# A positional-bias table for attention: order of its row groups, one-pass rows and early loads

## Chip, core and metric

The kernel runs on one core of one Trainium2 chip. The metric is the device time of one execution in microseconds (us). The core has a matrix engine (TensorE, PE in the rows), a vector engine (VectorE, DVE), a scalar engine (ScalarE, ACT), GpSimd (POOL) and a queue engine (SyncE, SP) that issues most transfers. Matmul results stand in PSUM, everything else on the chip in SBUF.

## What is computed

Attention with a learned positional bias, then a two-layer feed-forward block with a rational activation. Cut to what matters here:

```python
scores = scale * np.matmul(q, k.transpose(0, 1, 3, 2))        # B 4, H 8, S 576, D 64
psi_rel = np.log1p(np.abs(pos[:, None] - pos[None, :]))
psi_i = np.log1p(np.maximum(pos[:, None], 1.0))
x = (psi_rel / psi_i)[..., None]
bias = np.maximum(x @ w1 + b1, 0.0) @ w2                       # hidden 32, one value for each head
scores = scores + bias.transpose(2, 0, 1)[None]
attn = softmax(scores);  out = attn @ v
h = out @ w_in                                                 # 2304 x 512 @ 512 x 2048
P = a[0] + a[1]*h + a[2]*h**2 + a[3]*h**3
Q = 1 + abs(b[0])*abs(h) + abs(b[1])*h**2
result = (P / (Q + 1e-6)) @ w_out
```

The bias depends on the row i and on the distance |i-j| alone. With psi_i > 0 it is relu(w1 log1p(d) + b1 psi_i) @ w2 / psi_i.

## The kernel before

**Three stages.** First the bias table is made for all heads and written to DRAM (lines 571 to 680). Then attention runs in 72 steps over pairs of heads and batches, with the weights of the feed-forward block being split into high and low parts beside it. Then the feed-forward block runs (lines 701 to 884).

**The table.** The 576 rows i are cut into 36 *groups* of 16 rows (NROW). For a group n, `relu(n)` makes four *rows*: tiles of 128 partitions (32 hidden units times four values of i) by `dist(n)` columns, where `dist(n) = max(16n+16, 576-16n)` is the longest distance that the group needs, from 304 (the middle groups) to 576 (the first and the last). The letter in `ENG[n]` says who makes a row: D is one `tensor_scalar` on VectorE (line 617), A one activation on ScalarE (line 615). Before, a D row is max(x, -b), which lacks a constant; PE computes that constant once (`pc`, line 596), ScalarE copies it (`c8`), and it goes in as the bias of the activation below. Rows go through a ring of 18 tiles, and `relu` runs two groups ahead (LEAD).

For each group PE multiplies the four rows with the scaled w2 (`w28`, four 32-column parts that run side by side) into one PSUM tile `pb` of 591 columns (line 657). The PSUM tiles come from three slots, so group y waits until group y-3 has been read. ScalarE scales it into SBUF (`e`, line 663), and SP writes `e` (295.5 KB) to the table in DRAM (`tab<-e`, line 669). There are eight `e` tiles.

**From the table to attention.** The table of a pair of heads comes back in five *blocks* of 128 query rows (block c is the groups 8c to 8c+7, and block 4 has only the four groups 32 to 35). `load_bias(p, c)` issues three transfers for a block (line 261), and six for block 4: its 64 rows go to both halves of the partitions. `done` says behind which place y of the group order a block of the first pair is loaded. `step_a(0)` and `step_a(1)`, the first two attention steps, are issued between the last two groups (EARLY).

**A step of attention** on PE: scores `sc` (line 338), transposes `tp` of an earlier step (line 407), product with v `mx` (line 447). VectorE adds the bias block to `sc` and takes the row maximum (`s`, line 348), and ScalarE takes the exponential (`p`, line 364). The steps go (unit 0, block 0), (0, 1), (0, 2), (1, 0), (1, 1), (0, 3), (0, 4), ... `sc` has two PSUM buffers, both taken by one step, so step i+1 can't start on PE before `s` of step i has read. Unit 1 needs its own q and k (`q1`, `k1`): before, `loads(1)` issues them, and `v1`, from ScalarE's queue in `step_a(1)`.

Every engine takes its instructions in program order, and a wait holds up everything behind it on that engine. SP holds transfers in the order of the program too; each transfer has one of eight semaphores by turns, and waits until the transfer eight before it has landed.

## Time and profile before

| | us |
|---|---|
| median of 3 runs (lowest, highest) | 675.21 (674.49, 675.36) |
| the profiled execution | 675.17 |
| its span, first to last instruction | 673.4 |
| PE busy in the span | 665.0 (99%) |
| VectorE, ScalarE, GpSimd busy | 568.7, 484.3, 157.3 |
| mean granted clock of PE | 0.999 |

How the rows further down are read. A **stretch** row gives from:to in us from the start of the span, its length, then busy time (and count) of PE, PEld (PE's weight loads), DVE, ACT and POOL, PE's granted clock as a share of 2.4 GHz, the busy share of the 16 DMA engines, and GB/s. A **time line** row gives start, duration, engine, line, operation, what it writes<-reads, shapes and xcount; instructions of one kind in a row are merged, and the duration is then from the start of the first to the end of the last. In square brackets stands the engine's idle time before it and what ended that. Instructions of one engine overlap: the next starts before the one before it has ended. A **group** row gives line, engine, operation, shapes, count, then busy us, mean ns of one, and idle us before them. Engines with a q (SPq, ACTq) are their queues, issuing transfers. A **DMA** row ends with KB of one transfer and the median us from issue to landing. A busy PE is modelled, and is not PE at its peak.

### The profile page before, as it was taken

How to read it: one execution, taken by the hardware profiler on the slowest of the kernel's cores; microseconds unless marked ns; L12 is line 12 of the kernel's file. 1: busy time of each engine (PE TensorE's matmuls, PEld its weight loads, DVE VectorE, ACT ScalarE, POOL GpSimd, SP SyncE). 2: the span in 40 equal slices, each digit the busy share in tenths (PEclk: the TensorE clock that was granted, in tenths of full speed). 3: DMA queues.
4: the chain of work that ended last, by engine and by line, in shares of the span. 5: the costliest groups of instructions: out<-in, count | busy, mean ns of one | idle time of the engine just before them, and what ended most of it. 6: DMA issues, size and time to landing. Idle time of an engine off the chain costs nothing.

```text
span 673.4 us, 16639 instructions
## 1 busy us (share of the span) xinstructions
PE 665.0 (99%) x6468; PEld 575.2 (85%) x6468; DVE 568.7 (84%) x1072; ACT 484.3 (72%) x767; POOL 157.3 (23%) x117
## 2 busy tenths in 40 slices
PE   9998999999999999999999999999999999999997
PEld 5666888888888888999999999999999999999995
DVE  7985888888888896699999999998978787878776
ACT  6998889989888997676676767676655555555561
POOL 0000133334333232122222222222222222222221
PEclk9999999999999999999999999999999999999999
DMA  4997888698788974323635353679731212122021
GB/s 146 324 331 223 295 267 283 214 289 274 242 260 273 283 225 138 99 82 117 231 91 201 95 188 101 198 219 346 267 105 47 94 48 93 48 95 94 1 94 47
DMA packets 74702, 119.01 MB, mean 177 GB/s; under 512 B 11888, under 2 KB 33536, under 8 KB 74624
## 3 DMA queue, kind: packets, MB, share of 16 engines
q1 hardware_dynamic: 74048, 116.87, 53.1%
q10 hardware_dynamic: 576, 1.08, 0.6%
q8 instruction: 51, 0.84, 0.5%
q14 instruction: 27, 0.22, 0.1%
HBM read 79.17 MB, written 35.61 MB: 170 GB/s over the span
## 4 chain that ended last, share of the span: by engine, by line
PE 96%; DMA 2%; ACT 1%; issue 0%; DVEq 0%; DVE 0%; ACTq 0%
PE h L314 30%; PE o L793 29%; PE mx L447 13%; PE sc L338 12%; PE tp L407 5%; PE pb L657 5%; PE mx L407 1%; DMA k<-in_kt_dram 1%; DMA cst<-in_cst_dram 0%; DMA tab<-e 0%; ACT e L663 0%; ACT ring L615 0%; ACT p L364 0%; PE warm L597 0%; ACT pt L415 0%
## 5 line engine op out<-in xcount | busy, mean ns | idle before, releaser
L762 POOL TENSOR_TENSOR gl<-m,r 128x768 fp32r<-128x768 f32 x47 | 87.1, 1854 | 306.6 <-DVE m L755 281.9
L348 DVE CUSTOM_DVE_ANT_0 s<-sc,bias 128x576 f32<-128x576 f32 x144 | 103.2, 754 | 15.3 <-PE sc L338 10.1
L715 ACT ACTIVATE w<-h,babs 128x768 f32<-128x768 f32 x48 | 43.3, 902 | 99.5 <-PE h L314 99.5
L364 ACT ACTIVATE p<-s,m 128x576 f32<-128x576 f32 x144 | 110.7, 772 | 1.7 <-DVE m L348 1.1
L314 PE MATMUL h<-xh,wih 128*128 128x384 f32 x288 | 96.9, 336 | 0.0
L314 PE MATMUL h<-xh,wil 128*128 128x384 f32 x288 | 96.7, 336 | 0.0
L314 PE MATMUL h<-xl,wih 128*128 128x384 f32 x288 | 96.5, 335 | 0.0
L447 PE MATMUL mx<-pt,v 128*64 128x128 f32 (+1 forms) x1600 | 95.1, 267 | 0.0
L338 PE MATMUL sc<-k,q 64*128 64x288 f32 (+1 forms) x640 | 90.3, 426 | 2.2 <-DMA k<-in_kt_dram 1.5
L415 ACT COPY pt<-tp 128x1024 f32<-128x1024 f32 x72 | 72.6, 1008 | 24.8 <-PE tp L407 24.5
L793 PE MATMUL o<-wol,gh 128*128 128x512 f32 x216 | 84.7, 392 | 0.0
L793 PE MATMUL o<-woh,gh 128*128 128x512 f32 x216 | 84.6, 392 | 0.0
L447 PEld LDWEIGHTS mx<-pt,v 128*64 128x64 f32 x1600 | 78.5, 137 | 5.0 <-issue 0.2
L725 DVE SCALAR_TENSOR_TENSOR u<-w,babs,h 128x768 f32<-128x768 f32 x48 | 48.6, 1013 | 30.9 <-ACT t L716 30.9
L720 ACT ACTIVATE u<-u 128x768 f32<-128x768 f32 x48 | 40.7, 848 | 40.5 <-DVE u L725 40.5
L338 PEld LDWEIGHTS sc<-k,q 64*128 64x128 f32 (+1 forms) x640 | 49.5, 175 | 21.6 <-DVE m L348 6.9
L741 DVE SCALAR_TENSOR_TENSOR gh<-t,cst,r 128x768 fp32r<-128x768 f32 x48 | 48.7, 1015 | 9.5 <-ACT r L722 7.2
L314 PEld LDWEIGHTS h<-xh,wih 128*128 128x128 f32 x288 | 54.1, 188 | 1.8 <-issue 0.5
L314 PEld LDWEIGHTS h<-xl,wih 128*128 128x128 f32 x288 | 54.1, 188 | 1.3
L793 PE MATMUL o<-woh,gl 128*128 128x512 f32 x216 | 54.8, 389 | 0.0
L314 PEld LDWEIGHTS h<-xh,wil 128*128 128x128 f32 x288 | 54.0, 188 | 0.0
L748 DVE SCALAR_TENSOR_TENSOR m<-u,qc,gh 128x768 f32<-128x768 f32 x48 | 48.9, 1019 | 4.9
(79 smaller groups left out, 1270.3 us busy)
## 6 DMA issues: line engine op xcount, KB each, us to landing
tab<-e SPq DMA_DIRECT2D x36, 295.5 KB, 4.0
wx<-in_w_in_dram SPq DMA_DIRECT2D x16, 512.0 KB, 5.7
wx<-in_w_out_dram SPq DMA_DIRECT2D x16, 512.0 KB, 4.5
xr<-xd SPq DMA_DIRECT2D x7, 768.0 KB, 4.6
ws<-wh SPq DMA_DIRECT2D x20, 256.0 KB, 2.0
ws<-wl SPq DMA_DIRECT2D x20, 256.0 KB, 3.9
v<-in_vp_dram SPq DMA_DIRECT2D x15, 320.0 KB
bias<-tab SPq DMA_DIRECT2D x16, 288.0 KB, 4.0
```

Source lines behind the costliest of these rows:

```text
L314: T.matmul(hps[s][:, j, :TT], w[:, k, sl], x[:, k, :], start=(k == 0 and z == 0), stop=(k == KD - 1 and z == 2),)
L338: T.matmul(sc[i, j][o, a, :SH], q[r, x], k[r, a * SH:(a + 1) * SH], start=True, stop=True,)
L348: V.tensor_tensor_reduce(out=t.rearrange("p (a s) -> p a s", a=2), in0=sc.pop((i, j))[:, :, :SH], in1=bias[p][:, 5 * j + c, :].rearrange(" ...
L364: A.activation(out=prob[i][:, z * S:z * S + S], in_=t, func=AF.Exp, bias=m, scale=-1.0, accum_out=sums[u % 4][:, k:k + 1],)
L415: A.copy(out=t[:, 0:8].rearrange("p x (r s) -> p r x s", r=2), in_=ps)
L447: T.matmul(ps[y, o], vt[n][:, kc, y], t[:, 2 * kc + j if kc < 4 else 8, o], start=(kc == 0), stop=(kc == 4),)
L715: A.activation(out=w, in_=h, func=AF.Abs, scale=babs[:, 1:2])
L725: V.scalar_tensor_tensor(out=et(s, "u", 2), in0=rt[s, "w"], scalar=babs[:, 0:1], in1=hps[s][:, :, :TT], op0=ALU.add, op1=ALU.mult,)
L741: V.scalar_tensor_tensor(out=hi, in0=rt[s, "t"], scalar=abs_[:, 0:1], in1=rt[s, "r0"], op0=ALU.add, op1=ALU.mult,)
L748: V.scalar_tensor_tensor(out=m, in0=rt[s, "u"], scalar=qc, in1=rt[s, "gh"].bitcast(F32), op0=ALU.add, op1=ALU.mult,)
L762: eng.tensor_tensor(out=lo, in0=rt[s, "m"], in1=rt[s, "r0"], op=ALU.mult)
L793: T.matmul(po[n, c], l[:, j, c * P:(c + 1) * P], r[fp][:, j, :], start=(first and x is a), stop=(last and x is z),)
```

## The change

Five edits, all in the table stage and at its edge.

1. **Rows.** A D row is now max(x + b, 0), one `tensor_scalar` with two operations, and every row is complete. The constant (`pc`, `c8`, two small memsets and copies, the bias operand of `e`) is gone, and so is the second table `nts`; `bts` is made by VectorE.
2. **Who makes rows.** Groups with `dist` over 432 give all four rows to VectorE, those over 400 give one to ScalarE, the others two: 112 rows on VectorE and 32 on ScalarE, where there were 117 and 27.
3. **Order of the groups.** Before 0 to 15, 32 to 35, 16 to 31. Now a short group and a long one by turns, starting with the groups 16 and 17 and ending with 31, 24, 30, 25, 29, 26, 28, 27.
4. **Loads at the start.** The log table `lts` comes in two parts of 320 and 256 columns; `q0`, `k0`, `q1`, `k1` and `v0` are issued by SP right behind it, `v1` by SP at place 21.
5. **Loads of the bias blocks.** Before: block 0 behind place 10, 1 behind 18, 2 behind 30, 3 and 4 behind the last. Now: block 2 behind place 16, 0 behind 19, 4 behind 30, 1 behind 31, and 3 behind the last.

```diff
             def load_bias(p, c):
-                if c == 0:
+                if p not in bias:
...
             def loads(i):
                 g, c = divmod(i, UPG)
-                if i == 1:
-                    load_qk(1, nc.scalar)
-                    load_v(1, nc.scalar)
...
-                nc.sync.dma_start(out=lts, in_=ltab)
+                LCUT = 320
                 nc.scalar.dma_start(out=cs, in_=cst)
+                nc.sync.dma_start(out=lts[:, :LCUT], in_=ltab[:, :LCUT])
+                nc.sync.dma_start(out=lts[:, LCUT:], in_=ltab[:, LCUT:])
+                for u in range(2):
+                    load_qk(u)
+                load_v(0)
...
-                V.tensor_scalar(
-                    out=nts, in0=pts, scalar1=b1s, scalar2=-1.0, op0=ALU.mult, op1=ALU.mult
-                )
-                V.tensor_scalar(out=lts, in0=lts, scalar1=w1s, scalar2=None, op0=ALU.mult)
+                V.tensor_scalar(out=bts, in0=pts, scalar1=b1s, scalar2=None, op0=ALU.mult)
                 A.activation(out=w28, in_=cs[:, 8 + 5 * NG:], func=AF.Identity, scale=8.0)
-                A.activation(out=bts, in_=pts, func=AF.Identity, scale=b1s)
...
+                ENG = [
+                    "DDDD" if dist(n) > 432 else "DDDA" if dist(n) > 400 else "DDAA" for n in range(NG)
+                ]
...
                             V.tensor_scalar(
-                                out=r, in0=lts[:, :dist(n)], scalar1=nts[:, m:m + 1], scalar2=None,
-                                op0=ALU.max,
+                                out=r, in0=lts[:, :dist(n)], scalar1=bts[:, m:m + 1], scalar2=0.0,
+                                op0=ALU.add, op1=ALU.max,
                             )
...
-                done = {10: 0, 18: 1, 30: 2}
+                done = {16: 2, 19: 0, 30: 4, 31: 1}
...
-                    if y == 1:
-                        load_qk(0)
-                    if y == 4:
-                        load_v(0)
+                    if y == 21:
+                        load_v(1)
...
                     A.activation(
                         out=e, in_=pa.rearrange("p a s -> p (a s)")[:, :EW], func=AF.Identity,
-                        bias=c8[:, z:z + 1], scale=rts[:, n:n + 1],
+                        scale=rts[:, n:n + 1],
                     )
...
                     if y == NG - 1:
                         load_bias(0, 3)
-                        load_bias(0, 4)
```

**SP at the end of the table, before.** `e27` is the `e` tile of group 27, `tab2` the part of the table that block 2 reads, `bias0` the bias of the first pair of heads.

```order
L669 DMA tab3_70<-e26_797 128x591
L261 DMA bias0_393<-tab2_69 128x576
L261 DMA bias0_393<-tab2_69 128x512
L261 DMA bias0_393<-tab2_69 128x64
L669 DMA tab3_70<-e27_820 128x591
L669 DMA tab3_70<-e28_840 128x591
L669 DMA tab3_70<-e29_860 128x591
L669 DMA tab3_70<-e30_876 128x591
L669 DMA tab3_70<-e31_906 128x591
L261 DMA bias0_393<-tab3_70 128x576
```

The same place on SP in the changed kernel (x2 are two transfers in a row):

```order
L664 DMA tab3_69<-e30_797 128x591
L260 DMA bias0_511<-tab4_70 64x576 x2
L260 DMA bias0_511<-tab4_70 64x512 x2
L260 DMA bias0_511<-tab4_70 64x64 x2
L664 DMA tab3_69<-e25_823 128x591
L260 DMA bias0_511<-tab1_67 128x576
L260 DMA bias0_511<-tab1_67 128x512
L260 DMA bias0_511<-tab1_67 128x64
L664 DMA tab3_69<-e29_846 128x591
L664 DMA tab3_69<-e26_866 128x591
L664 DMA tab3_69<-e28_882 128x591
L664 DMA tab3_69<-e27_912 128x591
```

Block 4's six transfers have moved from behind the last group to a place five groups ahead of it, and block 1, which the second attention step reads, now stands behind them.

**ScalarE at the start of the table, before.** `ring` and `ring2` are row tiles, `pb0` is PE's result for group 0.

```order
L590 ACTIVATE w28_62<-cst_61 128x128
L591 ACTIVATE bts_137<-cst_61 128x144
L598 COPY c8_63<-pc_145 128x1
L599 COPY c8_63<-pc_145 96x1
L615 ACTIVATE ring_131<-lts_133,bts_137 128x576
L615 ACTIVATE ring_131<-lts_133,bts_137 128x560
L615 ACTIVATE ring2_132<-lts_133,bts_137 128x544
L663 ACTIVATE e0_184<-pb0_171,c8_63,cst_61 128x591
```

The same place on ScalarE in the changed kernel:

```order
L586 ACTIVATE w28_62<-cst_61 128x128
L612 ACTIVATE ring_130<-lts_132,bts_133 128x320 x2
L612 ACTIVATE ring_130<-lts_132,bts_133 128x304 x2
L658 ACTIVATE e16_188<-pb16_175,cst_61 128x591
L612 ACTIVATE ring2_131<-lts_132,bts_133 128x304 x2
L658 ACTIVATE e17_208<-pb17_195,cst_61 128x591
L658 ACTIVATE e0_228<-pb0_215,cst_61 128x591
L612 ACTIVATE ring_130<-lts_132,bts_133 128x320 x2
```

Three small instructions are gone from the head of ScalarE's queue, and its rows now come in pairs of short ones, with none between a short group's `e` and the long group's `e` behind it.

**ScalarE at the edge of attention, before.** `p0` is the exponential of step 0.

```order
L364 ACTIVATE p0_891,sum0_117<-s2_0_0_885,m0_0_886 128x576
L663 ACTIVATE e31_906<-pb31_893,c8_63,cst_61 128x591
L267 DMA q1_918<-in_qt_dram 128x576
L268 DMA k1_919<-in_kt_dram 128x576
L274 DMA v1_922<-in_vp_dram 128x640
L364 ACTIVATE p0_891,sum0_117<-s2_0_1_888,m0_1_889 128x576
```

In the changed kernel, ScalarE at the same place:

```order
L363 ACTIVATE p0_897,sum0_116<-s2_0_0_891,m0_0_892 128x576
L658 ACTIVATE e27_912<-pb27_899,cst_61 128x591
L363 ACTIVATE p0_897,sum0_116<-s2_0_1_894,m0_1_895 128x576
```

The three issues of unit 1's q, k and v have left ScalarE's queue; SP issues `q1` and `k1` at the very start.

## Rows read from the trace of the kernel before

**Rows 1.** The page, chain that ended last, share of the span by engine:

```profile
PE 96%; DMA 2%; ACT 1%; issue 0%; DVEq 0%; DVE 0%; ACTq 0%
```

**Rows 2.** Stretches: the table, attention from step 3, feed-forward, the end:

```profile
4.80:46.86 42.06, 41.96 (x840) 27.49 (x844) 42.04 (x117) 39.33 (x62) 0.45 (x1) 1.00 0.80 279
...
56.28:264.06 207.78, 207.78 (x3428) 173.00 (x3428) 176.21 (x530) 186.77 (x370) 66.71 (x53) 1.00 0.81 255
264.75:669.50 404.75, 404.73 (x2114) 367.27 (x2114) 343.84 (x407) 248.33 (x318) 88.53 (x48) 1.00 0.38 124
669.50:672.30 2.80, 0.00 (x0) 0.00 (x0) 0.86 (x2) 0.00 (x0) 0.00 (x0) 1.00 0.63 244
672.30:673.40 1.10, 0.00 (x0) 0.00 (x0) 0.00 (x0) 0.00 (x0) 0.00 (x0) 0.51 0.00 0
```

**Rows 3.** Time line of PE at the edge of attention:

```profile
50.24 1.32 PE L338 MATMUL sc<-k,q 64*128 64x288 f32 x8
52.33 1.67 PE L338 MATMUL sc<-k,q 64*128 64x288 f32 x7 [0.77 <-DVE m L348]
...
54.09 0.71 PE L407 MATMUL tp<-ident,p 64*128 64x64 f32 x13
56.28 1.24 PE L338 MATMUL sc<-k,q 64*128 64x288 f32 x8 [1.48 <-DMA k<-in_kt_dram]
...
59.25 1.24 PE L338 MATMUL sc<-k,q 64*128 64x288 f32 x8
```

**Rows 4.** Time line of VectorE at the edge of attention, step 1's first half:

```profile
51.51 0.76 DVE L348 CUSTOM_DVE_ANT_0 s<-sc,bias 128x576 f32<-128x576 f32 x1 [1.24 <-PE sc L338]
```

**Rows 5.** Time line of VectorE in the table stage:

```profile
4.04 0.29 DVE L586 TENSOR_SCALAR nts<-cst 128x144 f32<-128x144 f32 x1 [4.04 <-DMA cst<-in_cst_dram]
4.25 0.51 DVE L589 TENSOR_SCALAR lts<-lts,cst 128x576 f32<-128x576 f32 x1
4.80 42.04 DVE L617 TENSOR_SCALAR ring<-lts,nts 128x576 f32<-128x576 f32 x117
```

**Rows 6.** Groups of VectorE by shape, 0 to 50 us, longest and shortest rows:

```profile
L617 DVE TENSOR_SCALAR ring<-lts,nts 128x576 f32<-128x576 f32 x7 | 3.2, 520 | 0.0
...
L617 DVE TENSOR_SCALAR ring<-lts,nts 128x304 f32<-128x304 f32 x6 | 1.8, 386 | 0.0
```

**Rows 7.** Time line of ScalarE, start of the table:

```profile
8.82 0.84 ACT L663 ACTIVATE e<-pb,c,cst 128x591 f32<-128x591 f32 x1 [1.55 <-PE pb L657]
10.56 0.84 ACT L663 ACTIVATE e<-pb,c,cst 128x591 f32<-128x591 f32 x1 [0.90 <-PE pb L657]
11.30 0.71 ACT L615 ACTIVATE ring<-lts,bts 128x512 f32<-128x512 f32 x1
11.92 0.83 ACT L663 ACTIVATE e<-pb,c,cst 128x591 f32<-128x591 f32 x1
```

**Rows 8.** Time line of ScalarE, middle and end of the table:

```profile
30.98 0.61 ACT L615 ACTIVATE ring<-lts,bts 128x304 f32<-128x304 f32 x1
31.42 0.90 ACT L663 ACTIVATE e<-pb,c,cst 128x591 f32<-128x591 f32 x1
32.15 0.61 ACT L615 ACTIVATE ring<-lts,bts 128x304 f32<-128x304 f32 x1
...
43.49 0.95 ACT L663 ACTIVATE e<-pb,c,cst 128x591 f32<-128x591 f32 x1
...
46.14 2.42 ACT L663 ACTIVATE e<-pb,c,cst 128x591 f32<-128x591 f32 x3
```

**Rows 9.** Time line of SP's queue: a block of three, block 4 twice later:

```profile
9.69 0.32 SPq L669 DMA_DIRECT2D tab<-e  x1
...
44.97 1.29 SPq L261 DMA_DIRECT2D bias<-tab  x3
...
96.37 3.94 SPq L261 DMA_DIRECT2D bias<-tab  x6
...
150.47 4.20 SPq L261 DMA_DIRECT2D bias<-tab  x6
```

**Rows 10.** DMA issues from 44 to 46.9 us, the second of block 2's three:

```profile
bias<-tab SPq DMA_DIRECT2D x1, 256.0 KB, 4.5
```

**Rows 11.** Groups of PE by shape, 6.5 to 8 us, then 10.3 to 13 us:

```profile
L657 PE MATMUL pb<-ring,w 128*32 128x497 f32 x8 | 1.9, 1025 | 0.0
...
L657 PE MATMUL pb<-ring,w 128*32 128x465 f32 x8 | 1.0, 554 | 0.0
```

More of the change, by code (lines that the diff above doesn't have):

```diff
@@ L56, in tile_attn_moe @@
     w28 = cpool.tile([P, 4 * HID], F32, tag="w28", name="w28")
-    c8 = cpool.tile([P, 2], F32, tag="c8", name="c8")
     babs = cpool.tile([P, 2], F32, tag="babs", name="babs")
@@ L578, in tile_attn_moe @@
                 lts = tpool.tile([P, S], F32, tag="lts", name="lts")
-                nts = tpool.tile([P, NG * 4], F32, tag="nts", name="nts")
-                nc.sync.dma_start(out=lts, in_=ltab)
+                bts = tpool.tile([P, NG * 4], F32, tag="bts", name="bts")
+                LCUT = 320
                 nc.scalar.dma_start(out=cs, in_=cst)
-                bts = tpool.tile([P, NG * 4], F32, tag="bts", name="bts")
+                nc.sync.dma_start(out=lts[:, :LCUT], in_=ltab[:, :LCUT])
[3 more added lines that the diff above has]
+                load_v(0)
                 G.memset(qc, 1.0 + 1e-6)
                 G.memset(wmin, -8.0 * 0x38000000)
-                G.memset(c8, 0.0)
-                V.tensor_scalar(
-                    out=nts, in0=pts, scalar1=b1s, scalar2=-1.0, op0=ALU.mult, op1=ALU.mult
-                )
-                V.tensor_scalar(out=lts, in0=lts, scalar1=w1s, scalar2=None, op0=ALU.mult)
+                V.tensor_scalar(out=bts, in0=pts, scalar1=b1s, scalar2=None, op0=ALU.mult)
                 A.activation(out=w28, in_=cs[:, 8 + 5 * NG:], func=AF.Identity, scale=8.0)
-                A.activation(out=bts, in_=pts, func=AF.Identity, scale=b1s)
-                pc = ps_mx.tile([P, 2, 512], F32, tag="mx", name="pc")[:, 0]
+                for a, z in ((0, LCUT), (LCUT, S)):
+                    V.tensor_scalar(
+                        out=lts[:, a:z], in0=lts[:, a:z], scalar1=w1s, scalar2=None, op0=ALU.mult
+                    )
                 warm = ps_tp.tile([P, 2, 512], F32, tag="tp", name="warm")
                 for x in range(9):
-                    if x == 6:
-                        T.matmul(pc[:, 0:1], w28, b1s, start=True, stop=True)
                     T.matmul(warm[:, 0, 0:P], ident, ident, start=True, stop=True)
-                A.copy(out=c8[:, 0:1], in_=pc[:, 0:1])
-                A.copy(out=c8[0:96, 1:2], in_=pc[0:96, 0:1])
-                ENG = ["DDDD" if n % 4 == 3 else "DDDA" for n in range(NG)]
                 def dist(n):
                     return max(NROW * n + NROW, S - NROW * n)
+                ENG = [
+                    "DDDD" if dist(n) > 432 else "DDDA" if dist(n) > 400 else "DDAA" for n in range(NG)
+                ]
                 rows = {}
@@ L630, in tile_attn_moe @@
                 bg = in_order(bg, after)
-                order = [*range(16), *range(32, NG), *range(16, 32)]
-                done = {10: 0, 18: 1, 30: 2}
+                order = [16, 17, 0, 18, 1, 19, 2, 20, 3, 21, 4, 22, 5, 23, 6, 11, 7, 12]
+                order += [8, 13, 32, 14, 33, 15, 34, 9, 35, 10, 31, 24, 30, 25, 29, 26, 28, 27]
+                done = {16: 2, 19: 0, 30: 4, 31: 1}
                 for n in order[:LEAD]:
@@ L661, in tile_attn_moe @@
                     e = rpool.tile([P, EW], F32, tag="e", name=f"e{n}")
-                    z = 1 if ENG[n][3] == "A" else 0
                     A.activation(
                         out=e, in_=pa.rearrange("p a s -> p (a s)")[:, :EW], func=AF.Identity,
-                        bias=c8[:, z:z + 1], scale=rts[:, n:n + 1],
+                        scale=rts[:, n:n + 1],
                     )
```

## The prediction

> **What bounds the kernel now.** I read the page first. Of the chain that ended last, 96% is PE [rows 1], so the question is where PE waits. The stretches answer it. From 56.28 to 264.06, and again from 264.75 to 669.50, PE's busy time is the whole stretch, to 0.02 us [rows 2]: once the fourth score step has begun, nothing this change touches can be hidden or won. The start of that step, `sc` of step 3 at 56.28, carries the rest of the kernel behind it, so the time after is 675.17 plus or minus what this start moves. Next comes the time line of PE just ahead of it. Two idle pieces stand there: 0.77 before step 2, which waited for VectorE to read step 1, and 1.48 before step 3, which waited for `k1` [rows 3].
>
> The table stage itself is full on two engines. VectorE makes its 117 rows from 4.80 to 46.84 without a pause [rows 2, 5]. ScalarE waits 1.55 and 0.90 for PE at the start and then is busy to the end, 39.33 of the 42.06 us [rows 2, 7]. PE's busy time in this stretch is no evidence of a limit, being modelled. So a saving on one of the two engines alone gives little.
>
> **The change part by part.**
>
> *Rows on VectorE.* A row of 576 columns takes 520 ns, one of 304 takes 386 [rows 6], so 134/272 = 0.493 ns a column. The 117 rows have 51,488 columns, so (42.04 - 25.38)/117 = 0.142 us is the share of a row that doesn't depend on its length. The new plan has 112 rows and 51,808 columns: 15.9 + 25.5 = 41.5 us against 42.04. Does the second operation cost something? The trace has a two-operation `tensor_scalar` with a column operand and a constant, `nts`, of 144 columns: the next instruction starts 0.21 after it [rows 5], and the one-operation formula gives 0.142 + 0.071 = 0.21. So I count it at nothing. Its upper bound, twice the price of a column, is a rival below. The split of `lts` costs one more 0.142, so rows begin at 4.04 + 0.21 + 0.30 + 0.27 = 4.82, where they began at 4.80. VectorE could end 0.5 earlier.
>
> *Rows on ScalarE.* A row of 304 columns holds ScalarE for 31.42 - 30.98 = 0.44, one of 512 for 11.92 - 11.30 = 0.62; an `e` for 32.15 - 31.42 = 0.73 [rows 7, 8]. That is 0.177 a row and 0.865 ns a column. Before: 27 rows, 11,872 columns, 15.0 us. Now: 32 rows, 11,552 columns, 15.7 us. So ScalarE gets 0.6 more, and VectorE 0.5 less. The three small instructions that leave ScalarE's head stood in its wait for PE and were free.
>
> *Start.* The first groups are short and shared two and two, so their rows are there about 0.5 earlier: two rows of 0.3 or 0.45 on each engine in place of three of 0.43. The first `e`, at 8.82 before, comes at 8.3. The second stood 1.74 behind the first [rows 7], because PE still ran at half its clock: eight matmuls of 497 columns were busy for 1.9 us at 6.5, eight of 465 for 1.0 after 10.3 [rows 11]. So the second `e` comes at about 10.2. From there ScalarE has to do, up to the `e` of place 30, 29 of them at 0.73 = 21.2, and 25 rows with 9,264 columns = 12.4. That is 43.8, and about 0.4 more for the third group, a long one that ScalarE has nothing to bridge: **44.2**, where it was 43.49 [rows 8]. The last groups are long ones made by VectorE; ScalarE has one row of 432 columns left (0.55) and needs 5 x 0.73, so place 34 ends between 48.4 and 48.8 (PE's pace, about one us a group, decides). Before it ended at 46.14 + 2.42 = 48.56 [rows 8]. **The table stage therefore gains nothing**: from -0.2 to +0.3, and I take +0.3.
>
> *Early q, k and v.* `k1` will have landed long before step 3: the wait of 1.48 goes. The queue of SP is idle up to 9.69 [rows 9], so these loads cost no issue time there. They share the DMA engines with `cst` and `lts`; at worst that moves the start by some tenths, which I leave in the range. `v1` at place 21 has some 20 us to spare. Were nothing else changed, step 3 would start at 56.28 - 1.48 + 0.3 = 55.1, and the kernel would take 674.0.
>
> *Block loads.* Block 2 and block 0 have more than 10 us to land, and block 3 alone remains behind the last group, which is needed only at step 5. Here lies the cost. Step 1 adds **block 1**, and its load has moved from place 18 to place 31, behind the six transfers of block 4. Six of them take SP 3.94 and 4.20 at two later places, against 1.29 for the three of another block [rows 9]. An `e` is issued 0.87 after its start (8.82 to 9.69) [rows 7, 9]. So:
> - `e` of place 30 issued at 44.2 + 0.9 = 45.1, its issue done at 45.45;
> - block 4: 4.1, to 49.6;
> - the `e` of place 31, long ready, 0.45: 50.05;
> - block 1's second transfer starts 0.4 behind its first, 50.45, and lands 4.5 later (the same transfer of block 2, under the same traffic) [rows 10]: 54.95.
>
> Step 1's first half needs this transfer and the small one behind it. Before, it started at 51.51 [rows 4]; moved by the stage it would be 51.8; now it is about **55.0**. VectorE waits there with steps 1, 2 and everything else queued behind; PE holds `sc` of step 2 until VectorE has read step 1.
>
> *Sum.* From the start of step 1 on VectorE to `sc` of step 3 were 56.28 - 51.51 = 4.77 us, of which 1.48 was `k1` [rows 3, 4]. The other 3.29 is a chain of two reads and one score step and stays. Step 3 then starts at 55.0 + 3.29 = 58.3, 2.0 later than before. 675.17 + 2.0 = **677.2**. The profiled run lies 0.04 below the median of the runs, so no correction.
>
> The Trainium skill, DMA: Bandwidth & Descriptors, Rules for kernel authors, says that two transfers to disjoint halves of the partitions bring nothing over one of 128, since both spread over the same engines; it names no extra cost. By it alone block 4 would pass SP like any other block, which is the first rival's time, and the rows of block 4 speak against it.
>
> **Rivals.**
>
> 1. *Block 1 is not late.* If SP passed block 4 in the 1.29 of a block of three, all behind it would be 2.8 earlier, step 1 would start at 52.2, step 3 at 55.45: 674.3; at best 674.0, with nothing late. It decides for no loss from the point where block 1 lands before about 53.0 (56.28 - 3.29). For it: the wait of 4.5 us is from busy traffic, others land sooner. Against it: 3.94 and 4.20 are two places with the same six transfers. Chance 0.22.
>
> 2. *PE's clock falls in the gap.* The forecast leaves PE idle from about 51.9 to 55.8, nearly 4 us; the longest piece before was 1.48. After the last matmul of all, the granted clock stayed at 1.00 up to 672.3 and then was 0.51, the lower level [rows 2]. If it falls here too, the first steps run at half speed. At the start two groups paid about 0.9 each for it [rows 11], so 1.8: 679.0. The Trainium skill, TensorE: Matmul & The Clock Gate, Part 1, has the same rule, that the throttled state is the default and activity releases it; by it the gap is a risk and the shorter ones were not. No gap of this length lies inside this trace. Chance 0.18.
>
> 3. *Two operations cost a column twice.* Then VectorE needs 0.493 ns x 51,808 = 25.5 us more, nearly all of it on the path: about 700. The `nts` row speaks against it, though it is one short row with other operations. Chance 0.03.
>
> **How the numbers follow.** Forecast 677.2 with chance 0.57. Its own range is 676.2 to 677.8: a landing of 4.0 or less and a stage without loss at one end, a slow issue at the other. Of this, about a quarter lies within 0.2% of 675.2 (1.35 us, about what a measurement of this kernel can tell from no change: 673.9 to 676.6). Rival 1 splits: 0.09 faster, 0.13 same. Rivals 2 and 3 are slower. Faster 0.10, same 0.27, slower 0.63. The range from 673.9 to 679.3 takes in rivals 1 and 2 but for their tails and leaves out rival 3.
>
> **What will show it.** In the profile after: the sum of the row pass (about 41.5 us for 112 rows, the same 520 ns at 576 columns); the end of the last-but-one `e` near 48.7; block 4's six transfers on SP near 45.5 to 49.6, and block 1's behind them; VectorE idle before step 1 for some 3 us, ended by the load of `bias`; no wait for `k1`; `sc` of step 3 near 58.3, and no PE idle behind it. I am wrong if VectorE doesn't wait for a bias block, if the table ends more than 1 us away from 48.7, or if PE runs its first attention steps at half speed.

## The result, and the profile after

The changed kernel takes **679.71 us** (median of 6 runs, 679.21 to 682.15). The kernel before, run beside it on the same chip, takes 675.29 (674.49 to 676.41). The ratio is 1.0068, with a 95% interval from 1.0051 to 1.0086. So the change makes the kernel slower by some 4.5 us. The prediction had the sign, 677.2, but the result lies 0.4 us above the upper end of its range, and most of the missing 2.5 us comes from a place that it never looked at.

The profiled run of the changed kernel took 679.69 us, its span is 677.9. First the start and the whole of the row pass on VectorE, to be read beside [rows 5] and [rows 6]: the time line (start in us, length in us, engine, line, operation, tiles, count, idle time before and what ended it), then groups (count, busy us, mean ns).

```profile
3.67 0.29 DVE L585 TENSOR_SCALAR bts<-cst 128x144 f32<-128x144 f32 x1 [3.67 <-DMA cst<-in_cst_dram]
3.88 0.64 DVE L588 TENSOR_SCALAR lts<-lts,cst 128x320 f32<-128x320 f32 x2
```

The groups, with all shapes together, and then the longest shape alone:

```profile
L614 DVE TENSOR_SCALAR ring<-lts,bts 128x576 f32<-128x576 f32 (+17 forms) x112 | 41.6, 463 | 0.0
...
L614 DVE TENSOR_SCALAR ring<-lts,bts 128x576 f32<-128x576 f32 x8 | 3.6, 518 | 0.0
```

The rows cost what they cost before, 518 ns at 576 columns against 520, and the 112 of them last 41.6 us, where 41.5 was forecast. They begin 0.36 earlier, because `cst` lands at 3.67 and not at 4.04.

Next the edge between the table and attention. ScalarE's last-but-one `e` (place 34), SP's queue (the letter q behind an engine's name marks its issues of transfers), VectorE's step 1, and PE, in this order, to be read beside [rows 3], [rows 4], [rows 8] and [rows 9]:

```profile
45.88 0.75 ACT L658 ACTIVATE e<-pb,cst 128x591 f32<-128x591 f32 x1 [0.71 <-PE pb L653]
...
43.97 4.05 SPq L260 DMA_DIRECT2D bias<-tab  x6
48.13 0.53 SPq L664 DMA_DIRECT2D tab<-e  x1
48.71 1.40 SPq L260 DMA_DIRECT2D bias<-tab  x3
...
53.23 0.76 DVE L347 CUSTOM_DVE_ANT_0 s<-sc,bias 128x576 f32<-128x576 f32 x1 [4.78 <-DMA bias<-tab]
...
48.04 1.69 PE L337 MATMUL sc<-k,q 64*128 64x288 f32 x8
54.05 2.48 PE L337 MATMUL sc<-k,q 64*128 64x288 f32 x7 [4.32 <-DVE m L347]
...
60.94 1.24 PE L337 MATMUL sc<-k,q 64*128 64x288 f32 x8
```

Block 4's six transfers hold SP for 4.05 us, block 1 goes out behind them at 48.71, and VectorE stands idle for 4.78 us until it has landed. PE, which has nowhere to put the scores of step 2, stands for 4.32. When it goes on, the same scores last 2.48 us that lasted 1.67 in [rows 3]. The last line is `sc` of step 4, at 60.94; before it stood at 59.25.

The stretches tell the rest (PE busy with count, weight loads, VectorE, ScalarE, GpSimd, granted clock, DMA share, GB/s). The three of after are the idle piece, the scores and transposes behind it, and a long piece of the feed-forward block:

```profile
48.00:54.05 6.05, 1.73 (x17) 1.00 (x9) 1.27 (x5) 2.15 (x6) 0.00 (x0) 1.00 0.86 284
54.05:57.50 3.45, 3.45 (x25) 2.56 (x26) 1.73 (x5) 1.70 (x5) 0.00 (x0) 0.53 0.42 139
...
300.00:640.00 340.00, 340.00 (x1710) 307.44 (x1708) 295.09 (x347) 212.83 (x275) 76.44 (x42) 1.00 0.41 134
```

The last one of the kernel before:

```profile
300.00:640.00 340.00, 340.00 (x1720) 309.55 (x1720) 296.11 (x348) 212.68 (x274) 76.03 (x41) 1.00 0.41 134
```

From 54.05 to 57.50 the granted clock is 0.53, close to the lower of TensorE's two levels. And far from all that the diff touches, in 340 us in which PE is never idle in either kernel, 1710 matmuls fit where 1720 did. That is 0.58%, over the some 405 us of the feed-forward block 2.4 us. The starts in this block agree with it: its first matmul comes at 268.82 (before: 266.70), which is 2.1 us late, and its last at 673.62 (before: 669.10), which is 4.5 us late.

So there are two losses to explain: an edge that is 1.7 us late at step 4, and a feed-forward block that runs 2.4 us longer on the same instructions. Another 0.4 us comes in the attention steps between; it was not followed.

### The profile page after: what moved, and what is told of

Same layout as the page of the kernel before. It is cut to its first block, busy times and chain, and to the rows that moved or that the text cites. A ratio compares the mean times of both kernels' runs of the same rounds, so it can differ in the third digit from the quotient of the medians.

```text
span 677.9 us, 16639 instructions
## 1 busy us (share of the span) xinstructions
PE 667.6 (98%) x6466; PEld 576.8 (85%) x6466; DVE 570.6 (84%) x1068; ACT 481.9 (71%) x769; POOL 156.5 (23%) x116
## 4 chain that ended last, share of the span: by engine, by line
PE 91%; ACT 0%; DVEq 0%; issue 0%; DVE 0%; ACTq 0%
PE h L313 30%; PE o L787 29%; PE mx L446 13%; PE sc L337 12%; PE tp L406 5%; PE mx L406 1%; ACT pt L414 0%; PE mx L422 0%; DVEq L953 0%; ACT p L363 0%; DVE pre L808 0%; ACTq L414 0%
## 5 line engine op out<-in xcount | busy, mean ns | idle before, releaser
L337 PE MATMUL sc<-k,q 64*128 64x288 f32 (+1 forms) x640 | 92.6, 430 | 4.3 <-DVE m L347 4.3
L735 DVE SCALAR_TENSOR_TENSOR gh<-t,cst,r 128x768 fp32r<-128x768 f32 x48 | 48.7, 1015 | 9.5 <-ACT r L716 7.2
L787 PE MATMUL o<-woh,gl 128*128 128x512 f32 x216 | 56.2, 395 | 0.0
```

Of the source, the lines that this page charges most:

```text
L337: T.matmul(sc[i, j][o, a, :SH], q[r, x], k[r, a * SH:(a + 1) * SH], start=True, stop=True,)
L735: V.scalar_tensor_tensor(out=hi, in0=rt[s, "t"], scalar=abs_[:, 0:1], in1=rt[s, "r0"], op0=ALU.add, op1=ALU.mult,)
L787: T.matmul(po[n, c], l[:, j, c * P:(c + 1) * P], r[fp][:, j, :], start=(first and x is a), stop=(last and x is z),)
```

## The experiments

All times are medians in us; "before" is the kernel before, run in between on the same chip.

| kernel | time | before | ratio, 95% interval | `sc` of step 4 | matmuls in 300 to 640 us |
|---|---|---|---|---|---|
| e1_swap | 675.04 | 675.36 | 0.9994 [0.9979, 1.0008] | 56.15 | 1712 |
| e2_pad | 676.94 | 675.36 | 1.0012 [0.9995, 1.0029] | 61.04 | 1721 |
| e3_swap_pad | 672.80 | 675.36 | 0.9968 [0.9953, 0.9982] | 56.38 | 1722 |
| e4_before_loads | 674.75 | 675.36 | 0.9993 [0.9980, 1.0006] | 58.93 | 1720 |
| e5_bias_operand | 674.28 | 674.78 | 0.9978 [0.9961, 0.9994] | 57.91 | 1721 |
| e6_warm | 676.43 | 674.78 | 1.0014 [0.9999, 1.0029] | 59.95 | 1721 |
| e7_before_shift | 678.33 | 674.78 | 1.0038 [1.0021, 1.0055] | 62.37 | 1710 |
| e8_b4_last | 672.23 | 674.78 | 0.9944 [0.9921, 0.9966] | 56.20 | 1721 |
| e9_old_order | 672.75 | 675.15 | 0.9960 [0.9945, 0.9975] | 56.66 | 1721 |
| e10_shift64 | 672.27 | 675.15 | 0.9961 [0.9946, 0.9977] | 56.21 | 1720 |
| e11_c1_early | 672.43 | 675.15 | 0.9956 [0.9941, 0.9972] | 56.71 | 1721 |
| e12_shift_up32 | 674.58 | 675.15 | 0.9987 [0.9974, 0.9999] | 56.18 | 1713 |
| e13_right32 | 674.80 | 675.04 | 0.9992 [0.9979, 1.0006] | 56.59 | 1713 |
| e14_both32 | 674.73 | 675.04 | 0.9996 [0.9981, 1.0011] | 56.70 | 1713 |

### The two suspects, one by one and together

**e1_swap**, on the changed kernel:

```diff
-                done = {16: 2, 19: 0, 30: 4, 31: 1}
+                done = {16: 2, 19: 0, 30: 1, 31: 4}
```

> The changed kernel with the loads of bias blocks 1 and 4 exchanged: block 1 (three transfers) goes behind place 30 and block 4 (six transfers) behind place 31; nothing else differs. My theory: the 4.78 us that VectorE waited for block 1, with the stretch at half the granted clock behind it, is the price of block 4 standing ahead of block 1 on SP. Then VectorE's first part of step 1 starts near 49 us instead of 53.2, the granted clock stays at 1.0 there, the scores of step 4, at 60.94 us in the changed kernel, start near 56.0, and the run is about 5 us shorter than the changed kernel's 679.7: 674 to 675.5. Rival A, block 1 is only one of the things that are late: the wait returns at the next load (block 2, v of the first pair or block 3), and the run stays above 677. Rival B, the half clock is not due to the idle TensorE behind that wait: the wait goes and the clock still reads 0.5 for some 3 us, which leaves about 676.5.

675.04, 4.7 us less than the changed kernel. SP, VectorE at step 1 and PE at steps 2, 3 and 4 in its time lines:

```profile
44.11 1.44 SPq L260 DMA_DIRECT2D bias<-tab  x3
45.65 0.68 SPq L664 DMA_DIRECT2D tab<-e  x1
46.37 3.73 SPq L260 DMA_DIRECT2D bias<-tab  x6
...
49.29 0.76 DVE L347 CUSTOM_DVE_ANT_0 s<-sc,bias 128x576 f32<-128x576 f32 x1 [0.87 <-PE sc L337]
...
50.12 1.67 PE L337 MATMUL sc<-k,q 64*128 64x288 f32 x7 [0.40 <-DVE m L347]
...
52.52 1.67 PE L337 MATMUL sc<-k,q 64*128 64x288 f32 x7
...
56.15 1.24 PE L337 MATMUL sc<-k,q 64*128 64x288 f32 x8
```

Block 1 goes out at 44.11 ahead of block 4. VectorE waits 0.87 at step 1, and for PE, not for the block. The scores of step 2 last 1.67 again, the granted clock is 1.00 from 48 to 57.5 us, and step 4 starts at 56.15, 4.8 us earlier than in the changed kernel and 3.1 earlier than before. Neither rival holds. Block 1 behind block 4 costs all of the loss at the edge, and hides a gain of 3 us under it.

**e2_pad**, on the changed kernel:

```diff
     w28 = cpool.tile([P, 4 * HID], F32, tag="w28", name="w28")
+    c8 = cpool.tile([P, 2], F32, tag="c8", name="c8")
+    nc.gpsimd.memset(c8, 0.0)
```

> The changed kernel with one unused 8-byte tile put back where the removed constant c8 stood; it is only cleared at the start, by GpSimd. In the changed kernel every tile allocated behind it lies 32 bytes per partition lower than in the kernel before; with the tile put back they lie where they were. My theory: this shift alone makes the matmuls of the feed-forward block slower, by the 2.4 us by which its instructions fall behind from 230 us to the end. Then the mean start-to-start of its matmuls returns from 199.2 to 197.8 ns and the time is about 2.4 us under the changed kernel's 679.7, near 677.3. Rival: the drift comes from the different start time of the block or from what is in flight beside it; then it stays near 679.7.

676.94, and 1721 matmuls in the 340 us. The edge is as late as in the changed kernel (step 4 at 61.04), so the 2.8 us come from the feed-forward block alone. An unused tile of 8 bytes is worth 0.4% of this kernel: by the addresses in the built programs, 1,075 tiles lie 32 bytes lower with `c8` gone. Among them are the activations that the second product of the feed-forward block reads (`gh`, `gl`) and those of its weights that are carved out of the bias buffer (`wg`); the resident weights (`wih`, `wil` of the first product, `woh`, `wol` of the second), allocated from the other end, do not move.

**e3_swap_pad**, both edits:

> Both edits together: blocks 1 and 4 exchanged and the 8-byte tile put back. If both theories hold and the two parts add, 672 to 673, faster than the kernel before (675.3) by about 0.4%. If the gain of the exchange is given back by a later wait, at least 674.5; if the address has no part in it, the same time as with the exchange alone.

672.80: together the two edits take off 6.9 us, where one by one they took 4.7 and 2.8, so they add up to within 0.5. The loss of the change is these two things, and without them its parts make the kernel faster than before.

### The address, looked at by itself

**e7_before_shift**, on the kernel before:

```diff
-    fill = cpool.tile([P, 104], F32, tag="fill", name="fill")
+    fill = cpool.tile([P, 96], F32, tag="fill", name="fill")
```

> The kernel before with one padding tile of 416 bytes per partition made 32 bytes smaller, so that everything allocated behind it lies 32 bytes lower, as in the changed kernel; no instruction changes. If the address alone slows the feed-forward block: 675.3 + 2.0 to 2.4 = 677.3 to 677.7, with the mean start-to-start of the matmuls from 300 to 640 us at 199.1 instead of 197.8 ns. Rival: the drift needs something else of the change; then 675.3 and 197.8 ns.

The ratio of 1.0038 is 2.6 us (1.4 to 3.7), and the count falls from 1720 to 1710, as in the changed kernel, though no instruction differs from the kernel before. One group of PE's matmuls from 300 to 640 us shows where it goes. The kernel before:

```profile
L793 PE MATMUL o<-woh,gl 128*128 128x512 f32 x186 | 47.2, 389 | 0.0
```

e7_before_shift:

```profile
L793 PE MATMUL o<-woh,gl 128*128 128x512 f32 x181 | 47.2, 395 | 0.0
```

And e2_pad, which has the old addresses in the changed kernel:

```profile
L789 PE MATMUL o<-woh,gl 128*128 128x512 f32 x186 | 47.2, 389 | 0.0
```

A matmul of the second product takes 395 ns where it took 389 (in the changed kernel it is 395 too). (The median, 678.33, lies above the 677.3 to 677.7 that were expected. In its profiled run, the longest of the twelve, the wait for `k1` was 2.83 us instead of the 1.48 of [rows 3], which has nothing to do with the feed-forward block.)

In the kernel before, every tile that these matmuls read begins at a multiple of 64 bytes; 32 bytes lower none on the moved side does. Four more kernels ask whether this is the rule. They stand on e8_b4_last (below), where these tiles are all at such multiples: 1721 matmuls.

**e10_shift64** (`fill` of 88 columns) and **e12_shift_up32** (`fill` of 112):

> The kernel with the 8-byte tile and block 4 last, with the padding tile 64 bytes smaller: everything behind it 64 bytes lower than in the kernel before. If what counts is where the tiles lie within 64 bytes, the matmuls from 300 to 640 us keep 197.7 ns from start to start and the time 672.2. Rival: any move from the place of the kernel before costs; then near 199 ns or over and 674.5 or more.

> The kernel with the 8-byte tile and block 4 last, with the padding tile 32 bytes larger: everything behind it 32 bytes higher than in the kernel before. If the place within 64 bytes counts, this is the same place as in the changed kernel, 32 bytes lower: 199.0 to 199.2 ns from start to start from 300 to 640 us and 674.2 to 674.6. Rival: only a move downwards, or the changed kernel's own place, is slow: 197.7 ns and 672.2.

672.27 and 1720 matmuls for a move of 64 bytes, 674.58 and 1713 for one of 32 upwards. Both times came as the place within 64 bytes says, and neither rival did. (That it is 1713 here and 1710 in the changed kernel is no difference of place: e1_swap, with the addresses of the changed kernel, has 1712.)

**e13_right32** and **e14_both32** add to e8_b4_last and e12_shift_up32 the same edit at the other end:

```diff
-            G.memset(wpool.tile([P, 120], F32, tag="edge", name="edge"), 0.0)
+            G.memset(wpool.tile([P, 128], F32, tag="edge", name="edge"), 0.0)
```

> The kernel with the 8-byte tile and block 4 last, and in it the padding tile at the upper end of the memory 32 bytes larger: the resident weights and the inputs of every other feed-forward pass, which had stood at a multiple of 64 bytes like everything else there, lie 32 bytes lower; the activations gh and gl stay. Theory 1, each tile's own place within 64 bytes counts: slower, by an amount not known, since other tiles move than in the changed kernel; fewer than 1720 matmuls in the 340 us from 300 to 640. Theory 2, the place of a matmul's two operands relative to each other counts: gh, gl and the resident weights now differ by 32 bytes, as in the changed kernel: near 1710 matmuls in 340 us and 674.2 to 674.9.

> The same, with the lower tiles 32 bytes higher too: all operands of the feed-forward matmuls stand 32 bytes behind a multiple of 64, and none differs from another. Theory 2 (relative place): the pace of the tuned place returns, 1720 matmuls in 340 us and 672.2. Theory 1 (each tile's own place): slow, 1710 matmuls or fewer, 674.2 or more, and the loss of the two moves adds up.

The stretch from 300 to 640 us of e10_shift64, all tiles at multiples of 64:

```profile
300.00:640.00 340.00, 340.00 (x1720) 309.74 (x1719) 294.87 (x345) 211.92 (x272) 78.06 (x42) 1.00 0.40 133
```

That of e13_right32, the resident weights off:

```profile
300.00:640.00 340.00, 340.00 (x1713) 307.96 (x1712) 294.17 (x345) 210.43 (x271) 76.06 (x41) 1.00 0.41 133
```

That of e14_both32, all of them off alike:

```profile
300.00:640.00 340.00, 340.00 (x1713) 307.81 (x1712) 294.34 (x345) 210.33 (x272) 76.00 (x41) 1.00 0.41 133
```

Moving the other side costs the same 7 or 8 matmuls. Moving both brings nothing back, so the relative place is not it. But the two losses don't add up either, as the first theory had it. What the runs show is this: with all these tiles at a multiple of 64 bytes the pace is the fast one, and with either side or both 32 bytes off it is the same slow one. Why one side is enough is open; which single tile does it was not tried.

Nor can the place of a matmul's own two operands be the whole rule. The groups of PE from 300 to 640 us show which matmuls are slower, and which are not. The kernel before, with the carved weights:

```profile
L793 PE MATMUL o<-wg,gh 128*128 128x512 f32 x120 | 37.1, 390 | 0.0
```

The changed kernel:

```profile
L787 PE MATMUL o<-wol,gh 128*128 128x512 f32 x186 | 73.6, 396 | 0.0
L787 PE MATMUL o<-woh,gl 128*128 128x512 f32 x185 | 48.1, 395 | 0.0
L787 PE MATMUL o<-wg,gh 128*128 128x512 f32 x120 | 37.1, 390 | 0.0
```

e14_both32, with `wg` and `gh` both 32 bytes off:

```profile
L315 PE MATMUL h<-xh,wih 128*128 128x384 f32 x248 | 83.2, 336 | 0.0
L790 PE MATMUL o<-woh,gl 128*128 128x512 f32 x186 | 48.4, 395 | 0.0
L790 PE MATMUL o<-wg,gh 128*128 128x512 f32 x122 | 37.7, 390 | 0.0
```

In all six slow kernels the products with `woh` and `wol` take 394 to 396 ns instead of 389 to 392, while those with `wg` stay at 390 to 392 although `wg` and `gh` have moved in five of the six, and the first product (`h`) stays at 335 to 337. The 557 products with `woh` and `wol` in the 340 us, each 2 to 6 ns longer, make 2.2 us by estimate, and the 10 missing matmuls at 198 ns each are 2.0: this is where the loss lies. The products with `wg` are also the last of their pass and come in another order, so what sets them apart is open too.

### The half clock, priced apart

**e6_warm**, on e2_pad, block 1 still late; 19 multiplications without use fill TensorE's wait:

```diff
                     if y >= NG - EARLY:
                         step_a(y - NG + EARLY)
+                warm = ps_tp.tile([P, 2, 512], F32, tag="tp", name="warm2")
+                for x in range(19):
+                    T.matmul(warm[:, 0, 0:P], ident, ident, start=True, stop=True)
```

> The changed kernel with the 8-byte tile in place and 19 multiplications of the identity by itself (128x128, about 0.22 us each, 4.1 us in all, into a free buffer) put on TensorE between the scores of step 1 and those of step 2, where it waits 4.3 us for VectorE; block 1 stays late. Theory of two prices: the wait for block 1 costs about 3 us and the half clock behind it 1.7 to 2. Then the clock reads 1.0 throughout, the scores of step 2 take 1.67 us instead of 2.48, those of step 4 start near 59.2 instead of 61.0, and the time is about 1.8 us under the 676.9 of the kernel with the tile alone: 675.0 to 675.4. Rival: VectorE and ScalarE hold the chain there whatever TensorE's clock; then it stays at 676.5 to 677. If the multiplications last longer than the wait, step 2 moves back by that much.

PE's time line (each of the added matmuls stands twice in the count):

```profile
49.68 4.51 PE L678 MATMUL warm<-ident 128*128 128x128 f32 x38
54.12 1.43 PE L339 MATMUL sc<-k,q 64*128 64x288 f32 x8
...
59.95 1.24 PE L339 MATMUL sc<-k,q 64*128 64x288 f32 x8
```

The stretch behind them:

```profile
54.00:58.00 4.00, 3.80 (x40) 2.90 (x39) 2.01 (x8) 3.19 (x9) 0.00 (x0) 1.00 0.50 164
```

The clock stays at 1.00 and the scores go at full speed, but the time is 676.43 against 676.94, and relative to the kernel before no difference shows. From VectorE's start on step 1 to the scores of step 4 it is 7.13 us (52.82 to 59.95) where e2_pad has 7.72 (53.32 to 61.04): **0.6 us**, not 1.8. The multiplications also overran VectorE by some 0.5 us (the scores of step 2 start 1.30 behind VectorE's step 1, in e2_pad 0.82), so the half clock costs 0.6 to 1.1. e1_swap, at full clock without any added matmuls, needs 6.86 for the same way (49.29 to 56.15), the changed kernel 7.71 (53.23 to 60.94): 0.85, in between. That the rest of the slower scores hides beside VectorE and ScalarE fits the trace, where VectorE waits for ScalarE's `p` at step 2 in both kernels (1.66 us in e2_pad, 1.23 here), but was not tried apart.

### What the useful parts bring

**e8_b4_last**, on the changed kernel with the tile of e2_pad:

```diff
-                done = {16: 2, 19: 0, 30: 4, 31: 1}
+                done = {16: 2, 19: 0, 30: 1}
...
                     if y == NG - 1:
                         load_bias(0, 3)
+                        load_bias(0, 4)
```

> The kernel with the 8-byte tile, and block 1 behind place 30 as in the exchange, but block 4 behind block 3 after the last place, as in the kernel before. My theory: in the exchange's trace block 4's six transfers still hold the last four e on SP from 47.6 to 51.4 and so put block 3 off to 56.4, for which step 5 waits 1.68 us. Without them the last e leave near 49 and block 3 starts near 53.5 to 54; the wait at step 5 goes, block 4 lands ahead of step 6, and the time falls by 1 to 1.7 us from 672.8, to 671.1 to 671.8. Rival: block 4, now issued behind block 3 from about 56.5 on, is late for step 6, which waits instead: 672.5 or more.

VectorE's time line at step 5 in e3_swap_pad:

```profile
61.63 0.76 DVE L349 CUSTOM_DVE_ANT_0 s<-sc,bias 128x576 f32<-128x576 f32 x1 [1.68 <-DMA bias<-tab]
```

And in e8_b4_last:

```profile
60.54 0.76 DVE L349 CUSTOM_DVE_ANT_0 s<-sc,bias 128x576 f32<-128x576 f32 x1 [0.76 <-ACT p L365]
```

The mechanism is right: block 3 goes out at 53.09 and not at 56.39, and the wait is gone. The time, 672.23, is 0.4 above the expected piece and 0.6 below e3_swap_pad. It is the fastest kernel here, by 0.56% (0.34 to 0.79%) faster than the kernel before.

**e9_old_order**, on e8_b4_last, puts back the order of the groups, the split of the rows and the places of the loads of the kernel before:

> The kernel with the 8-byte tile and block 4 last, and in it the order of the row groups, the split of the rows between VectorE and ScalarE, and the places of the block loads of the kernel before: so the two-operation rows, e without its bias, the early constants and the early loads alone. What the new order and split are worth is the difference to the kernel with block 4 last (672.2). My theory: a little; the two of them bring the scores of step 0 from some 47.0 us to 45.6, and cost 0.5 us at step 1, where block 1 is the last of its three to be complete; with the old order block 1 is there and step 1 does not wait. Then scores of step 0 at 46.8 to 47.2, no wait of VectorE for a bias block, and 672.7 to 673.5. Rival: the order and the split gain nothing, the table is shorter through e and the constants alone; then the scores of step 0 start by 45.9 and the time is 671.5 to 672.2.

672.75, so the new order and the new split are worth 0.3 to 0.5 us (672.43 and 672.23 with them), about as little as these runs can tell. The expected scores of step 0 were wrong, though: they start at 46.16, not at 46.8 to 47.2. Nearly all of the gain comes from the other parts of the change.

**e5_bias_operand**, on e3_swap_pad:

```diff
-                        scale=rts[:, n:n + 1],
+                        bias=c8[:, 0:1], scale=rts[:, n:n + 1],
```

> The kernel with blocks 1 and 4 exchanged and the 8-byte tile in place, and ScalarE's e given a bias column again (all zeros, so nothing computed changes). My theory: the bias column is what made e cost 0.73 us from start to start in the kernel before against 0.64 in the changed one. Then e returns to 0.73, ScalarE takes 36 x 0.09 = 3 us more for the table, of which its idle time in the table (some 2 us) absorbs part: the scores of step 0 start 1 to 2.5 us later than 45.8 and the time is 673.5 to 675. Rival: e is faster for another reason (the uninterrupted clock, another neighbour on the PSUM port); then e stays at 0.64 and the time at 672.8.

ScalarE's time line in e3_swap_pad:

```profile
11.48 1.39 ACT L660 ACTIVATE e<-pb,cst 128x591 f32<-128x591 f32 x2
12.75 1.05 ACT L614 ACTIVATE ring<-lts,bts 128x336 f32<-128x336 f32 x2
```

And in e5_bias_operand:

```profile
11.32 1.57 ACT L660 ACTIVATE e<-pb,c,cst 128x591 f32<-128x591 f32 x2
12.78 1.04 ACT L614 ACTIVATE ring<-lts,bts 128x336 f32<-128x336 f32 x2
```

Two `e` take 12.75 - 11.48 = 1.27 without a bias column and 1.46 with one, 0.635 and 0.73 each. So the column costs 0.09 to 0.1 us, and for the price the expectation holds. The Trainium skill, ScalarE: Activation LUTs, What ACT_TABLE_LOAD costs, says the same: each column operand adds about 93 ns to an activation. But the scores of step 0 come only 0.4 us later (46.16 against 45.80), less than expected, since ScalarE otherwise waits for PE at the end of the table. Step 4 is 1.5 us later, because block 1 left SP at 46.13 instead of 44.78, and the time, 674.28, lies within the expected range. In the ratio to the kernel before the two kernels can't be told apart.

**e4_before_loads** puts the early loads alone on the kernel before:

> The kernel before with only the last part of the change: q, k of the first two units and v of the first are loaded ahead of the table, v of the second at place 21, and the loads on the ScalarE queue at step 1 are gone. By the prediction's term for this part, TensorE's wait for k of 1.48 us in front of step 3 goes and nothing is put in its place: 673.8 to 674.0, that is 1.3 to 1.5 us less than before. Rival: another wait of the same length stands there (the pt copy or the exponentials of step 2 on ScalarE), and the time stays within 0.3 us of before.

Neither expectation came true; the time is 0.6 us less, with an interval from 1.35 less to 0.4 more, while 1.3 to 1.5 less was expected. The wait for `k1` is gone, but step 4 starts only 0.3 us earlier than in [rows 3]. VectorE's start shows one reason:

```profile
4.63 0.29 DVE L586 TENSOR_SCALAR nts<-cst 128x144 f32<-128x144 f32 x1 [4.63 <-DMA cst<-in_cst_dram]
```

The loads of q, k and v that now go out ahead of the table put `cst` off from 4.04 to 4.63, and the whole table with it. In the changed kernel `cst` is issued first in the program and lands at 3.67. The other reason: from step 3 to step 4 it is now 3.65 us instead of 2.97, since the scores of step 3, 1.24 us long in [rows 3], are drawn out over 1.9 (55.28 to 57.19), as those of step 2 are in both kernels. The two take 0.6 and 0.7 of the 1.48.

**e11_c1_early**, on e8_b4_last, rewrites the second half of the order:

```diff
-                order += [8, 13, 32, 14, 33, 15, 34, 9, 35, 10, 31, 24, 30, 25, 29, 26, 28, 27]
-                done = {16: 2, 19: 0, 30: 1}
+                order += [8, 13, 9, 14, 10, 15, 32, 24, 33, 25, 34, 26, 35, 27, 31, 28, 30, 29]
+                done = {16: 2, 19: 0, 27: 1}
```

> The kernel with the 8-byte tile and block 4 last, with the second half of the order rewritten: groups 8 to 15, which make block 1, come by place 23, block 1 is loaded behind place 27, and the long groups 32 to 35 alternate with 24 to 27 after them. My theory: the last 0.5 us that TensorE waits in front of step 2 hangs on block 1's landing; with block 1 loaded earlier VectorE's 0.99 us wait at step 1 goes and the time is 671.5 to 672.0. Rival: the table itself becomes longer, because the last groups are less even, and this eats the gain: 672.2 or more, with the scores of step 0 later than 45.8.

The rival: block 1 goes out at 41.24 and VectorE no longer waits for it, but the scores of step 0 start at 46.26 instead of 45.63, and 672.43 is no better than 672.23.

## Why the prediction was wrong, step by step

*Rows.* Right: 41.6 us for 112, 518 ns at 576 columns; the second operation costs nothing, and rival 3 is out.

*The price of `e`.* Wrong: 0.64, not 0.73. I took the duration from a row of before without asking what the removed bias column was part of (e5_bias_operand).

*The start.* The first `e` comes at 7.37 and not at 8.3, the second at 8.90 and not at 10.2. ScalarE's time line, and the groups of PE from 5.5 to 7.2 us and from 7.2 to 12:

```profile
7.37 0.76 ACT L658 ACTIVATE e<-pb,cst 128x591 f32<-128x591 f32 x1 [1.18 <-PE pb L653]
...
8.90 1.38 ACT L658 ACTIVATE e<-pb,cst 128x591 f32<-128x591 f32 x2
...
L653 PE MATMUL pb<-ring,w 128*32 128x271 f32 x8 | 1.1, 644 | 0.0
L653 PE MATMUL pb<-ring,w 128*32 128x287 f32 x4 | 0.4, 403 | 0.0
...
L653 PE MATMUL pb<-ring,w 128*32 128x497 f32 x8 | 1.0, 582 | 0.0
```

I let PE run its first groups at half speed, as in [rows 11], where 497 columns take 1025 ns. In the changed kernel only the first eight matmuls are slow (271 columns, 644 ns, against 403 for 287 columns behind them), and the next of 497 columns take 582 ns. That the removed matmul of the constant, which interrupted the warm-up, was the cause was not tried.

*The end of the table.* Wrong by its own bound: place 34's `e` ends at 45.88 + 0.75 = 46.63, 2 us ahead of the 48.7 forecast. "The table stage therefore gains nothing" was the consequence of the two steps above.

*Block 1.* Right in kind: block 4 held SP for 4.05 us (4.1 forecast), VectorE waited, and TensorE behind it. Step 1 started at 53.23, not at 55.0: SP came to block 4 at 43.97 and not at 45.45, and to block 1 at 48.71 and not at 50.05. The wait was 4.78 and not 3: the 3 was what step 1 is late by, and leaves out the 1.24 for which VectorE stood idle there already [rows 4].

*From step 1 to step 3.* Mis-sized, with the half clock of rival 2 in it. PE's scores of step 3 begin here:

```profile
57.40 0.61 PE L337 MATMUL sc<-k,q 64*128 64x288 f32 x1
```

That is 57.40 - 53.23 = 4.17 us, not 3.29; e1_swap, at full clock, has 52.52 - 49.29 = 3.23. The half clock did come, behind 4.32 us without a matmul, though it had a chance of 0.18, but at 0.6 to 1.1 us, not at the 1.8 that I had for it. That PE "runs its first attention steps at half speed" was one of the signs of being wrong.

*Early q, k and v.* Mis-sized as well: the wait of 1.48 goes, but from step 3 to step 4 it is 3.54 us here and 3.63 in e1_swap, not the 2.97 of [rows 3], since the scores of step 3 are now drawn out (e4_before_loads).

*The sum at the edge.* These errors cancel. The forecast puts `sc` of step 4 at 58.3 + 2.97 = 61.3; it started at 60.94. With the address restored the kernel takes 676.94, and the forecast was 677.2. That is luck: a right number with three wrong terms in it, 1.8 us too late at step 1, 0.9 too little from there to step 3 and 0.6 too little from step 3 to step 4.

*What was left out.* That "once the fourth score step has begun, nothing this change touches can be hidden or won" is **the step that failed**. PE is busy without a pause there, but how long it is busy is not fixed: the change takes away a tile of 8 bytes, and 400 us of matmuls became 2.4 us longer by it (e2_pad, e7_before_shift). That puts 677 at 679.7. Why a move by 32 bytes makes these matmuls slower stays open. The kernel holds tiles that nothing reads, `fill`, `fill2` and `edge`; they could have been asked what they are for.

What went where, then: the useful parts bring 2.6 us (e3_swap_pad against its kernel before), block 1 behind block 4 takes 4.7 (e1_swap against the changed kernel), the address 2.8 (e2_pad). The sum is +4.9, and +4.4 was measured; the 0.5 between is that of e3_swap_pad, whose two edits together take off 6.9.

## What to carry to other kernels

A tile that is removed or resized moves all tiles that are allocated behind it: compare their addresses before saying that untouched code costs what it did. When a stage becomes shorter, what is issued on a queue in fixed order must be sorted by who needs it first; here three transfers behind six that were not urgent cost more than all other edits gained. And a cost taken from a row holds for the instruction with the same operands only.

## What the hardware showed that I had not expected

- When the tiles of the feed-forward block lie 32 bytes off a multiple of 64, on one side or on both, its fp32 matmuls of 512 columns with the resident weights `woh` and `wol` take 394 to 396 ns in the trace instead of 389 to 392, and 340 us hold 1710 to 1713 matmuls instead of 1720 to 1722, 0.4 to 0.6% fewer. Matmuls of the same shape with `wg`, 32 bytes off as well, and those of 384 columns do not slow down. A move of 64 bytes costs nothing.
- A bias column on an activation of 591 columns costs 0.09 to 0.1 us.
- TensorE's granted clock was 0.53 in the 3.45 us behind 4.32 us of idleness in the middle of the kernel, near the lower level, and 0.74 in 6 us behind an idle piece of 2.83. At the edge of attention the first of these cost 0.6 to 1.1 us.

The second is from e7_before_shift: PE's time line at step 3, then the stretch that begins there:

```profile
57.94 2.29 PE L338 MATMUL sc<-k,q 64*128 64x288 f32 x8 [2.83 <-DMA k<-in_kt_dram]
...
58.00:64.00 6.00, 6.00 (x72) 4.91 (x72) 2.19 (x7) 2.85 (x7) 0.00 (x0) 0.74 0.69 198
```
